# An attention and expert kernel planned over five engines: planned idle time of TensorE filled, single load buffers, timed priorities, and batch 0's q products turned by TensorE

## The chip, the cores and the metric

One core of a Trainium2 chip runs the whole program. The metric is the device time of one execution in microseconds (us), smaller is better. Times vary with the chip and from run to run, so a kernel is only compared with the kernel before on the same chip, in the same rounds.

Names of engines: PE is TensorE (matmul; PEld its weight load), DVE is VectorE, ACT is ScalarE, POOL is GpSimd, SP issues the DMAs. The time outside the profiled span is about 2 us (span 101.7 us in an execution timed at 103.5).

On one core a run is called "slow" when it is over 1.5% above the fastest run of the same kernel.

## The reference

```python
# q, k, v: (4 batches, 4 heads, 1088 rows, 32); S1, S2: (8, 32)
def phi(x):                                    # 64 features per head and row
    a = einsum('rd,bhsd->bhsr', S1, x)         # "sketch"
    b = einsum('rd,bhsd->bhsr', S2, x)
    return outer_product(a, b)                 # "product", 8 x 8
q_p, k_p = phi(q), phi(k)
kv  = einsum('bhsf,bhsd->bhfd', k_p, v)        # "k-v"
num = einsum('bhsf,bhfd->bhsd', q_p, kv)       # "numerator"
den = q_p . sum_s(k_p) + 1e-6
x   = (num / den), heads side by side          # (4, 1088, 128)
# then one expert of 8 for each batch:
e   = argmax(mean_s(x) @ w_gate); g = softmax(...)[e]          # "gate"
out = g * (relu(x @ w1[e]) @ w2[e])            # w1 128x1024, w2 1024x128
```

So each batch is a chain: load, turn, sketch, products, k-v, numerator, mean, gate, load of the chosen weights, cast, two expert products, store. Four batches are independent, which is what the kernel uses to keep the engines busy.

## The kernel before

Every step is an operation with a cost for each engine that may run it, a priority, the operations that it waits for and the buffers that it uses. A list scheduler in the program plays the plan through in simulated time and fixes, when the kernel is built, the order of instructions on each engine, which of two engines runs a flexible step, and which buffer it gets. Hardware then runs each engine's list in that order and waits on semaphores. `big` is a pair of PSUM banks, `small` one bank; a `small` is half of a two-bank tile.

```python
    kinds = dict(kld=2, qld=2, vld=2, kT=2, qT=2, ...)        # buffers of each kind
    banks = [psum.tile([P, 2, 512], FP32, name=f"ps{i}") for i in range(4)]
    def T(slot):
        if slot.kind == "big":
            return banks[slot.index]
        if slot.kind == "small":
            return banks[slot.index // 2][:, slot.index % 2, :]
        ...
    # in attention(b, pr): 
        both = {"DVE": 0.97, "POOL": 1.52} if FLEX[b] else {"POOL": 1.52}
        kp = [add(both, products(kab, phk, s), ...) for s in range(3)]
        ...                                                    # [cut]
        qtr = []
        for s in range(3):
            pq = add(both, products(qab, phq, s), after=[iv], ...)
            qtr.append(add({"DVE": 0.95}, lambda s=s: nc.vector.transpose(...), after=[pq], ...))
        ...                                                    # [cut]
        def logits():
            for i in range(3):
                nc.tensor.matmul(T(lgps)[:, 0:E], T(pool)[:, i:i + 1].to_broadcast([P, P]), wg[:, :],
                                 start=(i == 0), stop=(i == 2))
    ...                                                        # [cut]
    FLEX = (True, False, False, False)
    A = (0, 100, 200, 300)           # priorities: batch after batch,
    M = (400, 500, 600, 700)         # experts after all attention
    with tc.manual_schedule():
        for op in plan.order():
            op.run()
```

Names in the profile: `kld qld vld` loaded inputs, `kT qT` turned inputs, `kab qab` sketches, `phk phq` products, `phT` turned q products, `wq` the weights of the q sketch, `wf wbf` expert weights in fp32 and bf16, `hT` hidden, `ob` output rows. All PSUM tiles are `ps`.

## Time and profile before

| | before |
|---|---|
| time, median of 4 runs beside the result | 103.4 us (102.97 to 104.7) |
| span of the profiled execution | 101.7 us |
| busy: PE, DVE, ACT, POOL | 78.3, 69.3, 37.6, 37.9 us |
| first expert matmul | 47.78 us |
| last product on POOL ends | 62.7 us |

The page of the kernel before: busy times, then the span in 40 slices with each engine's busy share in tenths.

```profile
...
PE 78.3 (77%) x1625; PEld 57.8 (57%) x1625; DVE 69.3 (68%) x126; ACT 37.6 (37%) x86; POOL 37.9 (37%) x40
...
PE   5894891688509995695999899589899989999810
...
POOL 6023400009990009896699999000140300000000
...
PE 50%; DVE 14%; POOL 9%; ACT 8%; issue 7%; DMA 6%; SPq 1%; DVEq 0%; ACTq 0%
...
```

No engine is full over the span, PE comes nearest. The row of PE has weak slices up to the 19th and is 8 or 9 in nearly all after that; POOL has holes of zeros before slice 16. The last line is the chain that ended last: half PE, the rest hops between engines.

The windows view of the kernel before says the same in numbers; columns are the stretch, its length, busy time (instructions) of PE, PEld, DVE, ACT and POOL, then the granted clock of PE, the DMA share and GB/s.

```profile
...
5.00:33.00 28.00, 18.30 (x455) 14.05 (x467) 18.30 (x28) 2.83 (x9) 10.17 (x8) 1.00 0.75 191
47.80:97.10 49.30, 45.30 (x768) 33.39 (x768) 37.68 (x70) 28.18 (x59) 17.14 (x12) 1.00 0.38 106
...
```

From 47.8 to 97.1 us PE is the limit (45.3 of 49.3). From 5 to 33 us nobody is. The granted clock reads 1.00 in both stretches, although the same group of matmuls takes 1.6 times as long early as late (below); so I read PE's speed from durations. Counts of matmuls are those of the profile, which has two records for each fp32 matmul of the code.

The groups view of the kernel before: busy time and mean ns after the first bar, then the idle time of the engine just before these instructions and what ended it.

```profile
...
L316 POOL TENSOR_TENSOR phk<-kab 128x768 f32<-128x768 f32 x10 | 16.6, 1673 | 22.6 <-ACT kab L286 19.3 <-DVE kab L288 3.3
...
L381 PE MATMUL ps<-phk,vld 128*32 128x64 f32 x288 | 8.7, 268 | 4.8 <-POOL phk L316 3.8 <-issue 0.5 <-DVE wq L363 0.4
...
```

POOL sat idle 22.6 us before its products of k, 19.3 of it waiting for ACT's copy of a k sketch. The timeline of the kernel before shows why (columns: start, duration, engine, operation, out<-in, and in brackets the idle time before it with what ended it).

```profile
...
9.20 2.15 POOL L316 TENSOR_TENSOR phk<-kab 128x768 f32<-128x768 f32 x1 [3.32 <-DVE kab L288]
...
13.30 2.29 PE L328 MATMUL ps<-wq,qT 128*32 128x96 f32 x49
...
18.70 1.18 PE L328 MATMUL ps<-wq,qT 128*32 128x96 f32 x23 [3.11 <-issue]
...
20.43 2.15 PE L328 MATMUL ps<-s,kT 128*32 128x64 f32 x72
...
23.04 3.72 POOL L316 TENSOR_TENSOR phk<-kab 128x768 f32<-128x768 f32 x2 [11.69 <-ACT kab L286]
...
```

Batch 0's q sketch starts at 13.30, stops after 49 of its 72 matmuls for 3.11 us in which the profile shows nothing that PE waits for ("issue"), and goes on at 18.70. Batch 1's k sketch stands behind it in PE's order and runs at 20.43, so POOL waits from 11.35 to 23.04 us.

### The profile page before, as it was taken

How to read it: one execution, taken by the hardware profiler on the slowest of the kernel's cores; microseconds unless marked ns; L12 is line 12 of the kernel's file. 1: busy time of each engine (PE TensorE's matmuls, PEld its weight loads, DVE VectorE, ACT ScalarE, POOL GpSimd, SP SyncE). 2: the span in 40 equal slices, each digit the busy share in tenths (PEclk: the TensorE clock that was granted, in tenths of full speed). 3: DMA queues.
4: the chain of work that ended last, by engine and by line, in shares of the span. 5: the costliest groups of instructions: out<-in, count | busy, mean ns of one | idle time of the engine just before them, and what ended most of it. 6: DMA issues, size and time to landing. Idle time of an engine off the chain costs nothing.

```text
span 101.7 us, 3774 instructions
## 1 busy us (share of the span) xinstructions
PE 78.3 (77%) x1625; PEld 57.8 (57%) x1625; DVE 69.3 (68%) x126; ACT 37.6 (37%) x86; POOL 37.9 (37%) x40
## 2 busy tenths in 40 slices
PE   5894891688509995695999899589899989999810
PEld 2283690476306673693567766457568767777600
DVE  2538860099986478929987876936986877998220
ACT  3202000122001532018946384527655645555200
POOL 6023400009990009896699999000140300000000
PEclk9999999999999999579999999999999999999995
DMA  2999999972402600860000259138655722222231
GB/s 51 340 257 274 296 242 335 204 193 55 186 0 58 165 3 0 241 188 6 0 6 0 67 96 325 37 71 259 205 151 190 235 65 63 71 66 57 66 82 41
DMA packets 11023, 13.35 MB, mean 131 GB/s; under 512 B 1536, under 2 KB 9216, under 8 KB 11008
## 3 DMA queue, kind: packets, MB, share of 16 engines
q1 hardware_dynamic: 10784, 13.11, 47.3%
q8 instruction: 12, 0.20, 0.8%
q10 hardware_dynamic: 224, 0.01, 0.1%
q14 instruction: 3, 0.02, 0.1%
HBM read 10.89 MB, written 2.23 MB: 129 GB/s over the span
## 4 chain that ended last, share of the span: by engine, by line
PE 50%; DVE 14%; POOL 9%; ACT 8%; issue 7%; DMA 6%; SPq 1%; DVEq 0%; ACTq 0%
PE ps L540 16%; PE ps L328 13%; POOL phk L316 7%; PE ps L519 7%; PE ps L449 7%; DMA qld<-in_q_dram 6%; ACT hT L529 5%; PE ps L381 4%; DVE ob L553 3%; DVE phT L438 3%; DVE hT L531 3%; POOL phq L316 2%; PE ps L475 2%; PE ps L393 2%; SPq L299 1%
## 5 line engine op out<-in xcount | busy, mean ns | idle before, releaser
L316 POOL TENSOR_TENSOR phk<-kab 128x768 f32<-128x768 f32 x10 | 16.6, 1673 | 22.6 <-ACT kab L286 19.3
L529 ACT ACTIVATE hT<-ps 128x768 bf16<-128x768 f32 (+1 forms) x26 | 19.4, 774 | 12.9 <-PE ps L519 12.9
L540 PE MATMUL ps<-wbf,hT 128*128 128x128 bf16 (+1 forms) x288 | 19.0, 219 | 1.9 <-ACT gate L487 0.8
L540 PEld LDWEIGHTS <-hT 128*128 128x128 bf16 (+1 forms) x288 | 17.0, 99 | 5.7 <-issue 3.7
L531 DVE TENSOR_SCALAR hT<-ps 128x768 bf16<-128x768 f32 (+1 forms) x22 | 19.3, 908 | 1.0 <-PE ps L519 0.9
L519 PE MATMUL ps<-xbf,wbf 128*128 128x384 bf16 (+1 forms) x96 | 18.3, 317 | 1.3 <-ACT wbf L286 0.6
L316 POOL TENSOR_TENSOR phq<-qab 128x768 f32<-128x768 f32 x10 | 15.6, 1584 | 2.3 <-DVE qab L432 1.9
L328 PE MATMUL ps<-wq,qT 128*32 128x96 f32 x288 | 10.1, 311 | 4.1 <-issue 3.1
L553 DVE TENSOR_SCALAR ob<-ps,gate 128x384 f32<-128x384 f32 (+2 forms) x15 | 7.3, 507 | 7.8 <-PE ps L540 6.4
L381 PE MATMUL ps<-phk,vld 128*32 128x64 f32 x288 | 8.7, 268 | 4.8 <-POOL phk L316 3.8
L519 PEld LDWEIGHTS <-wbf 128*128 128x128 bf16 x96 | 8.6, 99 | 6.2 <-issue 1.5
L328 PEld LDWEIGHTS ps<-wq,qT 128*32 128x32 f32 x288 | 8.8, 144 | 5.8 <-issue 4.3
L438 DVE STREAM_TRANSPOSE phT<-phq 128x768 f32<-128x768 f32 x12 | 11.3, 959 | 0.5 <-POOL phq L316 0.5
L381 PEld LDWEIGHTS ps<-phk,vld 128*32 128x32 f32 x288 | 6.4, 137 | 7.0 <-POOL phk L316 4.6
L288 POOL CAST wbf<-wf 128x1024 bf16<-128x1024 f32 x3 | 3.6, 1210 | 15.1 <-DMA wf<-in_moe_w_dram 9.6
L449 PE MATMUL ps<-phT,kvs 32*32 32x256 f32 (+1 forms) x256 | 7.1, 463 | 0.6 <-DVE phT L438 0.6
L328 PE MATMUL ps<-s,kT 128*32 128x64 f32 x288 | 6.9, 267 | 0.8 <-DVE s L267 0.7
L288 DVE COPY qab<-ps 128x256 f32<-128x256 f32 (+1 forms) x4 | 1.7, 439 | 8.5 <-ACT qab L286 6.9
L286 ACT COPY qab<-ps 128x320 f32<-128x320 f32 (+1 forms) x4 | 1.6, 414 | 15.9 <-PE ps L328 15.9
L305 DVE STREAM_TRANSPOSE kT<-kld 128x576 f32<-128x576 f32 (+1 forms) x8 | 5.6, 729 | 2.0 <-DMA kld<-in_k_dram 2.0
L305 DVE STREAM_TRANSPOSE qT<-qld 128x576 f32<-128x576 f32 (+1 forms) x8 | 5.6, 720 | 2.0 <-DMA qld<-in_q_dram 2.0
L328 PEld LDWEIGHTS ps<-s,kT 128*32 128x32 f32 x288 | 6.0, 141 | 1.6 <-issue 0.8
(62 smaller groups left out, 71.3 us busy)
## 6 DMA issues: line engine op xcount, KB each, us to landing
wf<-in_moe_w_dram SPq DMA_DIRECT2D x8, 512.0 KB, 4.3
out_dram<-ob SPq DMA_DIRECT2D x40, 48.0 KB, 1.6
kld<-in_k_dram SPq DMA_DIRECT2D x3, 544.0 KB, 8.5
qld<-in_q_dram SPq DMA_DIRECT2D x3, 544.0 KB, 7.9
vld<-in_v_dram SPq DMA_DIRECT2D x8, 144.0 KB, 7.7
vld<-in_v_dram SPq DMA_DIRECT2D x8, 128.0 KB, 6.7
kld<-in_k_dram SPq DMA_DIRECT2D x1, 288.0 KB, 2.9
qld<-in_q_dram SPq DMA_DIRECT2D x1, 288.0 KB, 4.6
```

The lines of the kernel that those rows point to most:

```text
L288: (nc.vector if eng == "DVE" else nc.gpsimd).tensor_copy(o, i)
L305: return [add({"DVE": 0.05 + 0.04 * 2 * n}, lambda a=a, n=n: nc.vector.transpose(out=T(tr)[:, 0:n, a:a + 2, :].rearrange("p c a t -> p a c ...
L316: (nc.vector if eng == "DVE" else nc.gpsimd).tensor_tensor(out=T(ph)[:, 3 * s:3 * s + 3, :, :].rearrange("p c h (i j) -> p (c h) i j", i=R ...
L328: nc.tensor.matmul(T(ps)[32 * a:32 * a + 32, c // n, w * (c % n):w * (c % n) + w], T(tr)[:, c, a, :], moving)
L381: nc.tensor.matmul(T(kvps)[32 * h:32 * h + 32, 0:64], T(vld)[:, h, c, :], T(phk)[:, c, h, :], start=(c == 0), stop=(c == NC - 1))
L438: qtr.append(add({"DVE": 0.95}, lambda s=s: nc.vector.transpose(out=T(phT)[:, :, 3 * s:3 * s + 3, :].rearrange("p f c t -> p c f t"), in_= ...
L449: nc.tensor.matmul(T(nps[a // 2])[32 * h:32 * h + 32, a % 2, 0:32 * LEN[a]], T(kvs)[32 * a:32 * a + 32, u, h, :], T(phT)[32 * a:32 * a + 3 ...
L519: nc.tensor.matmul(T(hp)[:, t, 0:w], T(wbf)[:, 0, 128 * j:128 * j + 128], T(xbf)[:, 384 * s:384 * s + w])
L529: nc.scalar.activation(out=o, in_=i, func=AF.Relu)
L531: nc.vector.tensor_scalar(out=o, in0=i, scalar1=0.0, scalar2=None, op0=MAXOP)
L540: nc.tensor.matmul(T(ops)[0:n, 128 * i:128 * i + 128], T(hT)[:, j, 128 * i:128 * i + n], T(wbf)[:, 1, 128 * j:128 * j + 128], start=(j == ...
L553: nc.vector.tensor_scalar_mul(T(ob)[0:n, lo:hi], T(ops)[0:n, lo:hi], g[0:n])
```

## The change

The intent: fill TensorE's planned idle time, use single load buffers, give each stage of each batch a tuned priority, and let TensorE turn batch 0's q products. The diff is long and holds more than its title says. Its core, with cuts marked:

```diff
-    kinds = dict(kld=2, qld=2, vld=2, ...
+    kinds = dict(kld=1, qld=1, vld=1, ...
                                             # [cut: the plan doubles PE costs before 8 us, adds 0.15 for a
                                             #  change of tile form, and models instruction pages of 256]
-                for a in range(4):          # k sketch: 72 matmuls into 32 rows
-                    nc.tensor.matmul(T(ps)[32 * a:32 * a + 32, ...], T(tr)[:, c, a, :], moving)
+                for o in range(0, P, m):    # 36 into 64 rows (m = 64); q sketch as before (m = 32)
+                    nc.tensor.matmul(T(ps)[o:o + m, ...], t[:, o:o + m], moving)
-        both = {"DVE": 0.97, "POOL": 1.52} if FLEX[b] else {"POOL": 1.52}
+        either, pool_only = {"DVE": 1.16, "POOL": 1.52}, {"POOL": 1.52}
+                if eng == "DVE" and ps is not None:     # one operand read from PSUM, not SBUF
+                    for c in range(3 * s, 3 * s + 3): ...
                                             # [cut: q products scaled straight out of PSUM, half of the q copies]
-            qtr.append(add({"DVE": 0.95}, ... nc.vector.transpose(...
+            tq = add({"PE": 0.7}, turn, ...)            # batch 0: 128-wide TensorE turns
+            te = add({"ACT": ..., "DVE": ...}, copy(eng, T(pT)..., T(tps)...))
+            nm = add({"PE": 0.66}, num, ...)            # numerator chunk by chunk
-            for i in range(3):                          # logits
-                nc.tensor.matmul(T(lgps)[:, 0:E], T(pool)[:, i:i + 1]...
+        sm = add({"DVE": 0.1}, ... reduce_sum(T(pool)[:, 3:4], ...))
+        lg = add({"PE": 0.3}, ... one matmul ...)
                                             # [cut: expert weights loaded and cast by halves; the first
                                             #  expert product waits for its own chunk of x alone]
-    FLEX = (True, False, False, False)
-    A = (0, 100, 200, 300)
-    M = (400, 500, 600, 700)
+    PT = (True, False, False, False)
+    FK = (False, True, False, True)
+    K = (-3.42, 23.86, 57.18, 51.88)        # [cut: nine more lines of tuned numbers]
+    def filler():
+        nc.tensor.matmul(T(wslot)[:, :], warm[:, 0:128], warm[:, :])
+    idle = plan.idle(ops, FILL)
-        for op in plan.order():
+        for op in ops:
             op.run()
+            for _ in range(int((idle.get(op, 0.0) - 0.1) / (0.43 if op.start < plan.COLD else 0.215))):
+                filler()
```

In the changed kernel's order there are 14 fillers.

## The prediction

> **What bounds it now.** Two stretches. From 47.8 us to 97.1 us TensorE is the limit: the windows view shows it busy 45.3 of 49.3 us, and the chain of waits runs mostly through the two expert products (24 second-product matmuls take 1.45-1.5 us, eight first-product ones 1.2-1.4). Before that nothing is full: from 5 to 33 us PE is busy 18.3 of 28, DVE 18.3, POOL 10.2. The chain there hops between loads, POOL and PE. POOL, which needs 32 us for its 20 feature products, idles 22.6 us before its phk products, 19.3 of it waiting for the ACT copy of the k sketch, and ends its last product at 62.7.
>
> PE is also slow there. The timeline shows 24 k-v matmuls in 0.87 us at 10-31 us and in 0.54 us from 40 us on; the k sketch takes 2.15 us at 5 and 20 us, about 1.3 us (estimate from 55 of 72 in 0.98) at 36 us. The Trainium skill, "TensorE: Matmul & The Clock Gate", Part 1, says an idle PE runs at half clock until some 3.4 us of sustained work; the trace's 1.6 times fits. PE further stops 3.1 us in the middle of a q sketch (15.6-18.7), waiting for nothing shown: probably instruction fetch queued behind loads (inferred).
>
> **What the change does.**
> - Fillers keep PE busy through planned gaps (14 dummy matmuls, 0.43 us cold, an estimated 0.22 warm) and should make PE warm from about 8 us instead of 33.
> - Single load buffers limit outstanding loads to three, so instruction pages queue behind less.
> - Timed priorities interleave batches. The order shows POOL nearly without holes (phk0, phk1, phq0, phq1, phk3/phk2, phq2, weight casts, phq3).
> - Batch 0 loses three DVE transposes (0.96 us each) and four DVE products (1.6-2.0 us each); gains PE transposes and three ACT copies of about 0.8 us. Two products (b1, b3) move to DVE reading one operand from PSUM. The Trainium skill, "SBUF — State Buffer", says a DVE instruction with two SBUF inputs contends with GpSimd reads; here POOL products took 2.2 us beside DVE's and 1.5 alone.
> - Three logits matmuls become one: about 4 x 0.5 us off PE.
>
> **Sum.** POOL starts at about 8; phk0 and phk1 to about 17, phq0 to 21.5. Batch 0 then needs turn, copy, numerator, gate (about 5 us) and weights plus cast (47.8 - 38.9 = 9 us before, some 8 now): first expert matmul at about 34.5, was 47.8. After it remain the expert work (12 x 1.48 + 12 x 1.33 = 34 us) and attention left over (q3, kv2, two numerators, turns, gates: about 8 us), plus 4 us of stalls as before, and the 4.6 us tail of eviction and store: 34.5 + 34 + 8 + 4 + 4.6 = 85 us of span, and 2 us between span and measured time: **87 us, 82 to 95**. Chances: faster by over 2% 0.94, within 2% 0.03, slower 0.03.
>
> **What would show it.** K-v groups of 0.54 us from before 15 us; no 3 us PE stop; POOL's last product before 48 us (62.7); first expert matmul at 31-38 us; from there PE over 90% busy; DVE busy 55-62 us (69.3), ACT over 42 us (37.6).
>
> **What would make it wrong.** PE cools again between fillers; instruction pages still stall it (more instructions early); single buffers starve POOL; ACT holds gate or weight copies behind others; fillers sit in front of work that is ready.

## The result, and the profile after

A ratio is the mean time of one kernel's fast runs over the mean of the other's fast runs of the same rounds, so it is not quite the ratio of the medians quoted beside it.

| | before | after |
|---|---|---|
| time, median of 4 runs each | 103.4 us | 93.91 us (93.49 to 94.58) |
| ratio of fast runs | | 0.910 (95%: 0.902 to 0.918) |
| span | 101.7 | 92.0 us |
| first expert matmul | 47.78 | 39.02 us |
| last product on POOL ends | 62.7 | 55.4 us |
| DVE busy | 69.3 | 56.7 us |

The page after, the same lines:

```profile
...
PE 76.6 (83%) x1453; PEld 55.5 (60%) x1456; DVE 56.7 (62%) x127; ACT 42.6 (46%) x89; POOL 37.8 (41%) x41
...
PE   4988999886999879969997989999869968899600
...
POOL 6022970999497999129922890040000000000000
...
PE 56%; DMA 13%; DVE 11%; POOL 6%; ACT 3%; issue 3%; SPq 3%; DVEq 0%; ACTq 0%
...
```

The windows view after, with the stretch that begins at its own first expert matmul:

```profile
...
5.00:33.00 28.00, 24.67 (x571) 18.99 (x572) 18.72 (x47) 8.37 (x27) 20.11 (x17) 1.00 0.63 188
39.00:87.40 48.40, 42.38 (x688) 30.84 (x688) 32.98 (x67) 30.37 (x55) 11.98 (x9) 1.00 0.45 118
...
```

Early PE went from 18.3 to 24.7 busy of 28 and POOL from 10.2 to 20.1. In the late stretch PE is busy 42.4 of 48.4, so it stands idle 6.0 us there.

The timeline after, early part:

```profile
...
5.58 0.23 DVE L289 TENSOR_TENSOR s<-ps,mask 128x64 f32<-128x64 f32 x1 [0.60 <-PE ps L677]
...
11.42 2.76 PE L365 MATMUL ps<-wq,qT 128*32 128x96 f32 x72
...
14.01 0.51 PE L417 MATMUL ps<-phk,vld 128*32 128x64 f32 x24
...
14.44 1.27 PE L365 MATMUL ps<-s,kT 128*64 128x64 f32 x36
...
16.16 2.98 POOL L352 TENSOR_TENSOR phk<-kab 128x768 f32<-128x768 f32 x2 [3.00 <-ACT kab L308]
...
19.10 1.51 POOL L352 TENSOR_TENSOR phq<-qab 128x768 f32<-128x768 f32 x1
19.52 0.19 DVE L399 TENSOR_TENSOR wq<-ps,mask 128x32 f32<-128x32 f32 x1 [1.09 <-PE ps L677]
...
```

The q sketch of batch 0 runs in one piece (2.76 us, no stop), the k-v group of 24 takes 0.51 us at 14.0 us (0.87 as late as 30 us before), and POOL waits 3.00 us for batch 1's k sketch where it waited 11.69. Two lines show a new cost: `s` and `wq` on DVE wait for L677, a filler.

The groups view after answers the two lines of before:

```profile
...
L352 POOL TENSOR_TENSOR phk<-kab 128x768 f32<-128x768 f32 x10 | 14.8, 1513 | 5.8 <-ACT kab L308 3.6 <-DVE kab L310 2.2
...
L417 PE MATMUL ps<-phk,vld 128*32 128x64 f32 x288 | 6.0, 228 | 2.1 <-POOL phq L352 0.7 <-DVE gate L567 0.7 <-DMA vld<-in_v_dram 0.4
...
```

From the PE groups of both profiles one can see where PE's own time went: the k-v groups fell from 8.7 to 6.0 us, the q sketches from 10.1 to 9.0, the logits from 3.1 to 1.5. Without warm-up (3.2 us in both) and fillers (3.9 us of records), PE worked 75.1 us before and 69.5 after; the rest of the span, in which it did nothing useful, fell from 26.6 to 22.5 us.

The timeline after, where batch 0 reaches its gate:

```profile
...
28.09 2.46 PE L365 MATMUL ps<-s,kT 128*64 128x64 f32 x72
...
30.47 0.39 PE L559 MATMUL ps<-wg,pool 128*128 128x8 f32 x2
...
31.52 0.17 DVE L565 MAX8 gate<-ps 128x8 f32<-128x8 f32 x1 [0.28 <-PE ps L391]
...
```

Batch 0's x (the input of its experts) is complete at 29.2 us, but its logits (L559) stand in PE's order behind 72 k-sketch matmuls of batches 2 and 3, and start at 30.47.

The waits view after, PE from 39 to 87.4 us (columns: us in total, times, longest), and the end of the timeline:

```profile
...
PE ps L631 <- ACT ob L641: 1.6, 3, 0.9
PE ps L631 <- DVE ob L644: 1.5, 2, 0.8
...
```

```profile
...
83.60 1.95 PE L631 MATMUL ps<-wbf,hT 128*128 128x128 bf16 x32
...
85.59 0.62 DVE L644 TENSOR_SCALAR ob<-ps,gate 128x384 f32<-128x384 f32 x1 [1.05 <-PE ps L631]
86.26 1.05 PE L631 MATMUL ps<-wbf,hT 128*128 128x128 bf16 x16 [0.71 <-DVE ob L644]
...
```

The second expert product (L631) waits for the eviction of the group before (`ob`), 0.71 us in the last case. The plan gives every group another PSUM bank, but after the change it alternates between the two banks of one tile, and the semaphores order accesses by tile. Before the change the plan rotated among four tiles.

### The profile page after: what moved, and what is told of

Read it like the earlier page. It is cut to its first block, busy times and chain, and to the rows that moved or that the text cites. A ratio compares the mean times of both kernels' runs of the same rounds, so it can differ in the third digit from the quotient of the medians.

```text
span 92.0 us, 3442 instructions
## 1 busy us (share of the span) xinstructions
PE 76.6 (83%) x1453; PEld 55.5 (60%) x1456; DVE 56.7 (62%) x127; ACT 42.6 (46%) x89; POOL 37.8 (41%) x41
## 4 chain that ended last, share of the span: by engine, by line
PE 56%; DMA 13%; DVE 11%; POOL 6%; ACT 3%; issue 3%; SPq 3%; DVEq 0%; ACTq 0%
PE ps L631 19%; PE ps L610 10%; PE ps L365 10%; DMA vld<-in_v_dram 7%; DMA qld<-in_q_dram 6%; DVE ob L644 5%; PE ps L417 5%; PE ps L505 4%; POOL phk L352 3%; POOL phq L352 3%; PE ps L533 3%; PE ps L540 2%; ACT ob L641 2%; SPq L321 1%; SPq L410 1%
## 5 line engine op out<-in xcount | busy, mean ns | idle before, releaser
L620 ACT ACTIVATE hT<-ps 128x768 bf16<-128x768 f32 (+1 forms) x30 | 22.0, 781 | 7.7 <-PE ps L610 7.7
L631 PE MATMUL ps<-wbf,hT 128*128 128x128 bf16 (+1 forms) x288 | 20.0, 219 | 3.8 <-ACT ob L641 1.6
L631 PEld LDWEIGHTS <-hT 128*128 128x128 bf16 (+1 forms) x288 | 17.8, 99 | 7.9 <-issue 6.0
L352 POOL TENSOR_TENSOR phq<-qab 128x768 f32<-128x768 f32 x12 | 17.8, 1514 | 6.7 <-DVE qab L483 6.7
L622 DVE TENSOR_SCALAR hT<-ps 128x768 bf16<-128x768 f32 (+1 forms) x18 | 16.2, 905 | 5.0 <-PE ps L610 4.9
L352 POOL TENSOR_TENSOR phk<-kab 128x768 f32<-128x768 f32 x10 | 14.8, 1513 | 5.8 <-ACT kab L308 3.6
L496 DVE STREAM_TRANSPOSE phT<-phq 128x768 f32<-128x768 f32 x9 | 8.4, 956 | 0.1
L417 PE MATMUL ps<-phk,vld 128*32 128x64 f32 x288 | 6.0, 228 | 2.1 <-POOL phq L352 0.7
L644 DVE TENSOR_SCALAR ob<-ps,gate 128x384 f32<-128x384 f32 (+2 forms) x10 | 4.7, 492 | 5.0 <-PE ps L631 4.9
L365 PEld LDWEIGHTS ps<-s,kT 128*64 128x64 f32 x144 | 5.4, 159 | 1.9 <-DVE s L289 1.2
L365 PE MATMUL ps<-s,kT 128*64 128x64 f32 x144 | 5.9, 248 | 0.3 <-DVE s L289 0.3
L308 ACT COPY kab<-ps 128x384 f32<-128x384 f32 (+1 forms) x6 | 2.2, 402 | 7.4 <-DVE kab L310 5.5
```

Of the source, the lines that this page charges most:

```text
L352: (nc.vector if eng == "DVE" else nc.gpsimd).tensor_tensor(out=T(ph)[:, 3 * s:3 * s + 3, :, :].rearrange("p c h (i j) -> p (c h) i j", i=R ...
L365: nc.tensor.matmul(T(ps)[o:o + m, c // n, w * (c % n):w * (c % n) + w], t[:, o:o + m], moving)
L417: nc.tensor.matmul(T(kvps)[32 * h:32 * h + 32, 0:64], T(vld)[:, h, c, :], T(phk)[:, c, h, :], start=(c == 0), stop=(c == NC - 1))
L496: turns = [add({"DVE": 0.95}, lambda s=s: nc.vector.transpose(out=T(phT)[:, :, 3 * s:3 * s + 3, :].rearrange("p f c t -> p c f t"), in_=T( ...
L620: nc.scalar.activation(out=o, in_=i, func=AF.Relu)
L622: nc.vector.tensor_scalar(out=o, in0=i, scalar1=0.0, scalar2=None, op0=MAXOP)
```

## The experiments

"Ratio" is that of medians over all rounds; the last column has that of the fast means.

| run | what | median us | fast mean | before: median, fast mean | ratio of medians | of fast means |
|---|---|---|---|---|---|---|
| nofill | after without fillers | 94.52 | 92.01 | 103.76, 100.29 | 0.911 | 0.917 |
| before_fill | before with fillers (wrong result) | 102.52 | 101.67 | same | 0.988 | 1.014 |
| fillapart | after, early results in tiles of one bank | 91.42 | 90.25 | same | 0.881 | 0.900 |
| apart | after, accumulators in tiles of one bank | 90.71 | 89.05 | same | 0.874 | 0.888 |
| after_again | after | 92.69 | 92.48 | 102.65, 99.60 | 0.903 | 0.929 |
| both_apart | both splits | 88.47 | 88.27 | same | 0.862 | 0.886 |
| oldprio | after with the old priorities | 92.53 | 91.60 | same | 0.901 | 0.920 |
| before_fill2 | before with fillers, mended | 103.67 | 99.02 | same | 1.010 | 0.994 |
| b0dve | oldprio, batch 0 back on DVE | 97.06 | 96.77 | 101.68, 100.41 | 0.955 | 0.964 |
| rot | after with load buffers doubled | 97.15 | 96.83 | same | 0.955 | 0.964 |
| unnamed | all the title's parts undone | 98.98 | 98.21 | same | 0.973 | 0.978 |
| bothapart_nofill | both splits, no fillers | 87.84 | 87.65 | same | 0.864 | 0.873 |

The changed kernel itself has 0.908 and 0.903 of medians, 0.910 and 0.929 of fast runs, so a difference of less than about 0.02 (2 us) says nothing. A theory and its rivals: I held at first that the order of the work (timed priorities and what the plan makes of them) made the gain; the rivals were the fillers and the warm clock, then the freed VectorE, the load buffers, and the small forms that the title does not name.

### nofill: do the fillers make the gain?

```diff
-            for _ in range(int((idle.get(op, 0.0) - 0.1) / (0.43 if op.start < plan.COLD else 0.215))):
-                filler()
```

> The changed kernel without its 14 filler matmuls; every other instruction and its order stay. Changed: 93.9 us. Theory CLOCK (the fillers buy PE's full clock early, and that is much of the gain): k-v groups of 24 take 0.87 us until 25 us or later instead of from 14 us on, q sketch of batch 1 2.7 us instead of 1.7, time 96 to 99 us. Rival ORDER (the order of work buys the gain, PE warms by the dense real work): k-v groups at 0.54 us from about 15 to 20 us all the same, time 92 to 94.5 us, perhaps below the changed kernel because s12 and wq no longer wait behind fillers (0.6 and 1.1 us in the changed trace).

Measured: 94.52 us, ratio 0.911, beside 0.908 and 0.903 for the changed kernel in its two series. Timeline of the kernel without fillers:

```profile
...
12.31 3.14 PE L365 MATMUL ps<-wq,qT 128*32 128x96 f32 x72
...
16.02 1.82 PE L365 MATMUL ps<-s,kT 128*64 128x64 f32 x36
...
```

PE is slow until about 17 us: the q sketch takes 3.14 us, the k sketch of 36 matmuls 1.82 where it takes 1.27 with the full clock. In the changed kernel's profile it came at about 14 us. But the moment varies without any change of fillers: the k sketch at 5.6 us took 2.19 us in the profile of the changed kernel and 1.27 in that of after_again, the same kernel; unnamed, which has no fillers, has 1.27 at 5.3 us, and bothapart_nofill, also without, has its fast k-v group of 0.51 us at 13.9. So that fillers bring the full clock forward is not shown. What is shown is that taking them out changes the time by less than the calls resolve.

### before_fill and before_fill2: fillers alone, on the kernel before

```diff
+    plan.add({"PE": 0.0}, lambda: None, after=[sts[1]["nm"]], prio=-30, uses=[wslot])
+            for _ in range(int((idle.get(op, 0.0) - 0.1) / (0.43 if op.start < plan.COLD else 0.215))):
+                filler()
```

> The kernel before with its order kept to the instruction on every engine, plus 37 filler matmuls in PE's planned gaps up to 30 us. Before: 103.4 us. Theory CLOCK: warm from about 14 us, 18 us of half-clock PE work before 33 us shrinks by some 6 us, of which half lies on the chain: 99 to 101 us. Rival ORDER: the early part is set by loads, POOL and waits; PE gets warm but the time stays within 1.5 us of 103.4.

before_fill gave a wrong result: my fillers went on writing after their PSUM bank had been given to other work. Its 102.52 us settles nothing. The mended kernel keeps the bank for as long as fillers run (28 of them):

> The kernel before with 28 fillers, mended: all of them ahead of the first numerator, so that none writes a PSUM bank that has been given to other work (the first attempt wrote on after that, and its result was wrong). Order kept on every engine. ORDER: 101.5 to 103.5 us with a correct result, k sketches at 1.2 us from about 16 us on where they took 2.15. CLOCK: 98 to 100.5.

Measured: correct, 103.67 us, ratio 1.010. Fillers alone gain nothing on the kernel before. Its timeline shows that the long stop stayed, and grew:

```profile
...
18.50 1.49 PE L334 MATMUL ps<-wq,qT 128*32 128x96 f32 x28 [4.52 <-issue]
...
23.58 1.51 POOL L322 TENSOR_TENSOR phk<-kab 128x768 f32<-128x768 f32 x1 [11.99 <-ACT kab L292]
...
```

PE had its full clock from about 11 us to the stop in this run (44 matmuls of the q sketch in 1.16 us, where before took 2.29 for 49), so it only reached its stop earlier. The stop is 4.52 us long, and after it the k sketch takes 2.15 us again, at the slow clock. POOL's products of batch 1 start at 23.58 (23.04 before).

### fillapart: do the fillers hold back work through a shared tile?

```diff
-    banks = [psum.tile([P, 2, 512], FP32, name=f"ps{i}") for i in range(4)]
+    # slots 0 and 1 (the fillers' bank and its neighbour): one-bank tiles until the first `big` use of pair 0
+    for j in (0, 1):
+        single[j] = fp.tile([P, 512], FP32, name=f"one{j}")
```

> The changed kernel with the fillers' PSUM bank in a tile of its own: same instructions, same order, but the DVE mask of s12, the DVE mask of wq and the ACT copy of zs no longer wait for fillers that write the other bank of the same tile. Theory SHARED TILE: s12 done at about 5.2 instead of 5.8 us, wq of batch 1 at 18.4 instead of 19.7, the first expert matmul 0.5 to 1.5 us earlier, time 92.5 to 93.5. Rival: POOL and the weights set the pace and nothing moves: 93.9 plus or minus 0.4.

Measured: 91.42 us, ratio 0.881 against 0.903 to 0.908. The order of instructions is unchanged. Timeline:

```profile
...
5.23 0.19 DVE L296 TENSOR_TENSOR s<-one,mask 128x64 f32<-128x64 f32 x1
...
16.41 0.18 DVE L406 TENSOR_TENSOR wq<-one,mask 128x32 f32<-128x32 f32 x1
...
17.44 1.69 PE L372 MATMUL ps<-wq,qT 128*32 128x96 f32 x72
...
```

The time is below the range that I gave (92.5 to 93.5). The two lines that waited for a filler after the change (`s` at 5.58, `wq` at 19.52) now stand at 5.23 and 16.41, without a wait. So the fillers did hold back work in the neighbouring bank. But most of these 3.1 us are not theirs, as PE was slow until 14 us in that profile and fast from about 10 in this one. after_again, the changed kernel with PE as fast as here (q sketch of 1.67 us at 10.5 in both), has `wq` at 17.65, waiting 1.26 us for a filler, and its first expert matmul at 38.09 us, fillapart at 36.81: about 1.3 us. The medians say 2 to 3. If the fillers only held work back by so much, nofill should have gained it; it did not, and in the split form (bothapart_nofill) taking them out costs nothing that would balance it. So the size stays open.

### apart: does the shared tile cost time in the expert stretch?

```diff
+    # after the last `big` use of pair 2: its two banks become two tiles
+                for j in (4, 5):
+                    single[j] = late.tile([P, 512], FP32, name=f"one{j}")
```

> The changed kernel with the two PSUM banks of the output accumulators as two tiles from the point on where they are used singly: same instructions, same order. In the changed trace PE waits 3.9 us for output evictions (1.6 ACT ob, 1.5 DVE ob, 0.4 pool, 0.4 before the logits), though the matmul that waits writes the other bank. Theory SHARED TILE: these waits fall below 1 us, PE over 92% busy from 39 us on (87.6% now), time 90.5 to 92. Rival (PE would wait anyway, for the relu copies that feed it): time 93.5 plus or minus 0.5, the waits reappear under hT.

Measured: 90.71 us, ratio 0.874. The waits of L631 for `ob` are gone from the list, and PE is busy 39.9 of 42.1 us from 39 us to its last matmul. Its profiled run also had a full clock from 5.4 us on, which belongs to the run and not to the edit, so of the difference in single profiles not all is the edit's; the medians over six runs are what counts.

### both_apart beside the changed kernel again: do the two add up?

> The changed kernel itself, on the chip of the other runs of this call, as their yardstick. Every theory: 93.9 us give or take 1; its fast runs at 0.91 of those of the kernel before.

> The changed kernel with both PSUM pairs as separate tiles (the fillers' pair early, the accumulators' pair late), order kept. The first runs gave about 2.5 us for the one and 3.3 for the other, in medians. Theory SHARED TILE (two separate causes, in separate stretches): the savings add, 88 to 89.5 us. Rival (the chip and the clock of those runs were luckier): 91 to 93 us.

Measured on one chip: 92.69 and 88.47 us (fast means 92.48 and 88.27), so 4.2 us, in the range of the theory that they add, though less than the 5.8 us that I had put together from the first runs. In the same place of the timeline as above:

```profile
...
77.58 2.84 PE L640 MATMUL one<-wbf,hT 128*128 128x128 bf16 x48
...
79.12 0.62 DVE L653 TENSOR_SCALAR ob<-one,gate 128x384 f32<-128x384 f32 x1 [0.31 <-DMA out_dram<-ob]
...
```

The 48 matmuls of the last two groups run through in one piece, while DVE evicts the first of them beside. The result is correct. The first expert matmul comes at 37.39 us and PE is busy 40.9 of the 44.3 us after it.

### oldprio: do the tuned priorities make the gain?

```diff
-    K = (-3.42, 23.86, 57.18, 51.88)     # and the nine other lines of tuned numbers
+    K = (0, 100, 200, 300)               # numbers of the kernel before, in the new places
```

> The changed kernel with the priorities of the kernel before (each batch 100 after the last, experts from 400, second products right after their first, w and v loads as before); fillers, single load buffers, TensorE turns and the planner's new costs stay. Theory ORDER: most of the 9.5 us goes, 98.5 to 102 us, POOL's last product after 55 us, first expert matmul after 42 us. Rival (the smaller mechanisms, products out of PSUM, turns on TensorE, one logits matmul, make the gain): 94 to 96.5 us.

Measured: 92.53 us, ratio 0.901 (after_again 0.903). My theory fell here (98.5 us or more), and the time is below the rival's range too (94 to 96.5). With the plain priorities of before, everything else as changed, the time is the same. The order does differ (first expert matmul at 41.50 instead of 39.02 us), and is worth nothing in the end: PE waits 1.1 us for `ob` in its list, 3.5 after the change; its profile fell in a slow run, so I take no more from it. Whether the tuned priorities gain something once the tiles are split was not run.

### rot: do single load buffers gain anything?

```diff
+        if slot.kind in ("kld", "qld", "vld"):       # two buffers in turn; order of every engine kept
+            if not hasattr(slot, "half"):
+                turns[slot.kind] = turns.get(slot.kind, -1) + 1
+                slot.half = turns[slot.kind] % 2
+            return bufs[slot.kind][slot.half]
```

> Edit: the changed kernel with the order of every engine kept, but each load buffer (k, q, v) doubled and used in turn, so a load no longer waits for the turn of the batch before it. Theory LOADS (single buffers gain by keeping few loads in flight, so that loads land in 4 us instead of 8 and instruction fetch is not held up): loads land in 6 us or more, a stop of 1.5 us or more in the middle of a PE group comes back before 30 us, time 95.5 us or more, ratio to before 0.93 or more. Rival (single buffers gain nothing, they save memory only): ratio 0.895 to 0.915, as the changed kernel, and k loads of batches 1 to 3 issued earlier.

Measured: 97.15 us, ratio 0.955 of medians and 0.964 (0.957 to 0.972) of fast runs. All of what the theory of the loads said came: k, q and v loads land in 7.1, 6.2 and about 5.5 us (4.9, 3.7 and about 3.6 after the change), and the stop is back. Timeline:

```profile
...
12.84 1.20 PE L372 MATMUL ps<-s,kT 128*64 128x64 f32 x33
...
18.23 0.33 PE L372 MATMUL ps<-s,kT 128*64 128x64 f32 x3 [4.18 <-issue]
...
18.99 1.51 POOL L359 TENSOR_TENSOR phk<-kab 128x768 f32<-128x768 f32 x1 [5.56 <-ACT kab L315]
...
```

Batch 1's k sketch starts at 12.84, 1.6 us earlier than in the changed kernel because this run's clock was full, and stops before its last 3 matmuls for 4.18 us. POOL gets it at 18.99 (16.16 after the change), the first expert matmul comes at 42.50 us (39.02). PE's useful work was even less than in the changed kernel (65.9 us: 73.9 less 3.2 warm-up and 4.8 fillers), the time it did nothing useful was 29.0 us instead of 22.5. So having the second load buffers costs 3 to 5 us (96.83 less the fast means 93.97 and 92.48 of the changed kernel, or the ratios of medians 0.955 less 0.903 and 0.908), through the stop, and not because the loads themselves come late: the turns of batch 1's k start at 11.44 us here and 11.07 in the changed kernel.

The DMA view of this run for 15 to 16 us, inside the stop:

```profile
...
q1 hardware_dynamic: 127, 0.26, 105.9%
q8 instruction: 1, 0.02, 8.0%
...
```

The load queue takes the whole time of the 16 engines in this microsecond, and one transfer of instructions lies in it. The kernel before has the same picture at 15 to 16 us, inside its own stop. That the stop is PE waiting for its next page of instructions behind the loads fits this and is likely; the profile does not name the receiver of the page, so it is argued and not shown. One more thing speaks for it: the place of the stop. The windows view from 0 to just before the stop, of before, before_fill2 and rot in this order, counts what PE and PEld had done:

```profile
...
0.00:18.69 18.69, 11.93 (x222) 7.99 (x222) 9.00 (x15) 2.26 (x5) 4.42 (x18) 1.00 0.95 253
...
0.00:18.49 18.49, 11.35 (x222) 6.25 (x222) 9.19 (x15) 2.26 (x5) 4.42 (x18) 0.96 0.94 267
...
0.00:18.22 18.22, 10.37 (x222) 6.50 (x222) 8.44 (x20) 2.40 (x5) 6.74 (x20) 1.00 0.93 267
...
```

All three stop after 222 weight loads and 222 matmuls, though they are then at different work (49 or 44 matmuls into a q sketch, 33 into a k sketch); unnamed and apart stop (2.41 and 0.54 us) after 222 weight loads and 221 recorded matmuls. The later stops of 1.3 to 1.8 us in rot, apart, fillapart, both_apart and bothapart_nofill (at 35.9 to 41.6 us) all come after 730 weight loads; bothapart_nofill has 14 fillers fewer than both_apart and stops 14 matmuls further into the same group. A place that is fixed in the count of instructions, and not in the work, is what a page of instructions would give. The first transfer of the queue `instruction` after the start begins at 15 to 17 us in before, before_fill2, rot and unnamed, just before 12 us in the changed kernel, which passes the same place without a stop. What is shown over all runs: in the first 25 us the kernels with double load buffers stop 3.1 (before), 4.5 (before_fill2), 4.2 (rot) and 2.4 us (unnamed), and 1.4 in before_fill; the single-buffered ones with the old tiles (after, nofill, after_again, oldprio, b0dve) 0.4 us or less. With single buffers and split tiles there are still stops of 0.3 to 1.8 us, most of them later.

### b0dve: does freeing VectorE of batch 0 make the gain?

```diff
-    PT = (True, False, False, False)
+    PT = (False, False, False, False)
-        kp = [add(either if FK[b] else pool_only, products(kab, phk, s, kps), ...
+        kp = [add(both if b == 0 else ..., products(kab, phk, s, kps if FK[b] else None), ...
+        # the same for qp; on top of the old priorities
```

> Edit: the old-priorities version of the changed kernel (92.5 us, ratio to before about 0.90), and batch 0 given back to VectorE as before the change: its k and q products free to go to DVE or POOL from SBUF (the plan puts two phk and two phq products on DVE), its q products turned by DVE in 32 blocks, no TensorE turns, no copies of turns by ACT. Fillers and single load buffers stay. Theory RELIEF (freeing VectorE of batch 0 makes the gain; DVE busy went from 69.3 to 56.7 us): at least 97 us, ratio to before 0.95 or more, POOL products at 2.1 us beside DVE's, first expert matmul at 44 us or later. Rival FORMS (the many small things make it: logits in one matmul, weights loaded and cast by halves, products scaled straight out of PSUM, two k products of batches 1 and 3 on DVE from PSUM): at most 94.5 us, ratio at most 0.925, first expert at 43 us or earlier. In favour of the rival: TensorE turns cost PE 2.6 us which this run saves.

Measured: 97.06 us, ratio 0.955 of medians, 0.964 (0.955 to 0.972) of fast runs; oldprio had 0.901 of medians and 0.920 of fast runs, so the ratio rose by 0.054 or 0.044, about 5 us. Timeline:

```profile
...
20.10 1.09 DVE L346 TENSOR_TENSOR phk<-ps,kab 128x256 f32<-128x256 f32 x3 [1.70 <-ACT kab L308]
...
20.15 1.51 POOL L352 TENSOR_TENSOR phk<-kab 128x768 f32<-128x768 f32 x1 [8.51 <-ACT kab L308]
...
21.54 3.13 DVE L352 TENSOR_TENSOR phq<-qab 128x768 f32<-128x768 f32 x2
21.70 2.16 POOL L352 TENSOR_TENSOR phq<-qab 128x768 f32<-128x768 f32 x1
...
```

The four lines show the two forms. DVE's product of batch 1 (L346, one operand from PSUM, three instructions) takes 1.09 us beside a POOL product of 1.51. Batch 0's on DVE (L352, both operands in SBUF) take 3.13 us for two (0.95 for the first, 2.27 for the second, which overlap in the records), and the POOL product beside them 2.16. This agrees with the Trainium skill, "SBUF — State Buffer", § Who interferes with whom: a DVE instruction with two SBUF inputs contends with a GpSimd instruction that reads SBUF, one with at most one does not.

In time the theory of relief held, in its mechanism only in part. I had expected batch 0 itself to be late, with a first expert matmul at 44 us or later; it came at 39.61. The loss lies behind it: the stretch from there to 92.0 us is 52.4 us long with 46.5 us of PE work (48.4 and 42.4 after the change). While POOL idles 8.51 us and is slowed, less of the later batches' attention is done before the experts begin. This run also has 26 fillers and another order, and its profile fell in a slow run, so the 5 us belong to the package of batch 0, not to one instruction. A part of POOL's wait is even the fillers': batch 1's k sketch is done at 17.9 us, but ACT waits 2.25 us, to 19.09, for a group of five of them at 17.80 before it gets to the copy that POOL needs.

### unnamed: all that the title names undone at once

```diff
-    kinds = dict(kld=1, qld=1, vld=1, ...
+    kinds = dict(kld=2, qld=2, vld=2, ...
     # and no fillers, old priorities, batch 0 on DVE as in b0dve
```

> Edit: everything that the change's title names is undone at once in the changed kernel: no fillers, load buffers doubled, old priorities, batch 0 back on DVE (products free between DVE and POOL, turns by DVE). What stays is what the title does not name: 64-wide k sketch, one logits matmul, q products scaled straight out of PSUM with half the copies, expert weights loaded and cast by halves, first product waiting for its chunk alone, k products of batches 1 and 3 free to go to DVE from PSUM, new costs in the plan. Theory NAMED (the four named parts together make the gain): 100 us or more, ratio to before 0.97 or more. Rival FORMS (the unnamed parts make it): 96 us or less, ratio 0.935 or less. Between the two: both have a share, which is then read off as the distance to 1 and to 0.905.

Measured: 98.98 us, ratio 0.973 of medians, 0.978 (0.969 to 0.987) of fast runs. It falls between the two theories, nearer to the one of the named parts. Of the distance from 1 to 0.905, 0.068 of 0.095 or about 70% goes with the named parts, and some 2 to 3 us stay with the small forms. Since fillers and priorities gained nothing when each was undone alone, the named parts that count are the load buffers and batch 0. Each alone is worth about 5 us, both together about 7: they overlap. A likely reason is that both make POOL wait for batch 1's k sketch (5.56 us in rot, 8.51 in b0dve, 9.29 here, 3.00 in the changed kernel).

### bothapart_nofill: do fillers help when they block nothing?

> Edit: the version with its PSUM accumulators and its early small results in tiles of one bank each (88.5 us, ratio to before 0.862), order kept, without its 14 fillers. Theory (fillers do help once they no longer hold back work on the neighbouring bank: without them the clock is full later, as in the run without fillers, where it came at 17 us): ratio 0.88 or more, about 90.5 us; k sketch at 5 us 1.8 us or longer and k-v groups of 0.87 before 15 us. Rival (fillers are worth nothing in either form): ratio 0.855 to 0.87, 87.5 to 89 us.

Measured: 87.84 us, ratio of medians 0.864 (both_apart 0.862). The full clock does come later in this profile, as the first theory had it (k sketch at 5.35 us 2.19 us, k-v 0.87 at 10.99; in the profile of both_apart 1.27 and 0.87), but the time is in the range of the rival. The ratio of fast runs, 0.873 (0.866 to 0.880), lies between the two ranges; but both_apart has 0.886 by the same measure, so nothing points to a gain from the fillers. I read this as: a worth of the fillers is not shown. The simplest version that beats both kernels is this one: the changed kernel with split tiles and without fillers, about 4 us below the changed kernel.

## Why the prediction was right or wrong, point by point

The time was inside the range, 93.9 for a point of 87.0, and the direction was right. Of the signs: k-v groups of 0.54 us before 15 us (right, 0.51 at 14.0); no 3 us stop (right); POOL's last product before 48 us (wrong, 55.4); first expert matmul at 31 to 38 us (wrong, 39.0); from there PE over 90% busy (wrong, 42.4 of 48.4 is 88%); DVE 55 to 62 us (right, 56.7); ACT over 42 us (right, 42.6).

**The sum.** "34.5 + 34 + 8 + 4 + 4.6 = 85 us of span" came out as 39.0 + 42.4 + 6.0 + 4.6 = 92.0. The work term was right (42 for 42.4). Two terms were mis-sized:

- "First expert matmul at about 34.5" was 39.0. Batch 0's q products ended at 23.56, not 21.5: POOL started at 8.71 instead of about 8, and it waited 3.00 us for batch 1's k sketch, which stands behind batch 0's q sketch in PE's order: "POOL nearly without holes" was read from the order of POOL alone. From there to the gate it took 8.5 us and not "about 5": the logits stood 1.1 us behind 72 sketch matmuls of other batches, and the evictions are three in a row. The weights took 7.0 and not 8.
- "4 us of stalls as before" was 6.0. The second product waits for `ob` of the group before, through a tile shared by two banks. An order list does not show this wait, as it does not tell which banks share a tile. Taking it and the early shared tile away gives 88.5 us, near to the 87 of the sum, though not by the sum's terms: the first expert matmul is still at 37.4 us and not at 34.5.

**The causes.** "Fillers ... should make PE warm from about 8 us instead of 33": PE was warm from about 14 us in the profile of the changed kernel and from about 5 in after_again, but runs without fillers spread as widely (5 to 17 us), so the clock part is not shown; and as a cause of the gain it was wrong, as nofill (0.911), before_fill2 (1.010) and bothapart_nofill show. PE's speed was not what the early stretch waited for. "Timed priorities interleave batches": they do, and oldprio shows that this is worth nothing here. "Single load buffers limit outstanding loads to three, so instruction pages queue behind less": right in its effect (the page of instructions stays inferred), and under-weighted: rot shows 3 to 5 us. "Batch 0 loses three DVE transposes and four DVE products": right as a large part, about 5 us in b0dve, though the loss without it falls in later batches. "Three logits matmuls become one: about 4 x 0.5 us off PE": PE's logits fell by 1.6 us; it was not tested alone.

What the Trainium skill, "TensorE: Matmul & The Clock Gate", Part 1, says of a cold and a warm PE agrees with the traces in direction (24 k-v matmuls in 0.87 and then 0.51 to 0.54 us, a ratio of 1.6 and not 2), also that the moment varies from run to run: with the same order of instructions the k sketch at 5.4 to 5.9 us took 2.19 (after), 1.90 (fillapart) and 1.27 us (apart, both_apart, rot).

What stays open: that the stop is an instruction page of PE (its place in the count of instructions speaks for it); how large the hold-back by the fillers is; how the 5 us of batch 0 divide into POOL's slowing, the DVE transposes and the order; and which of the unnamed forms hold the last 3 us.

## What to carry to other kernels

Before filling an engine's idle time ask what the stretch waits for: on the kernel before, PE had its full clock at 11 us instead of 33 (but for the time from its stop to about 24 us) and the time did not move, while in the changed kernel undoing the single load buffers, or the relief of VectorE from batch 0, cost 3 to 5 us each. Where semaphores follow tiles, two accumulators in one tile are one buffer; give each its own tile before tuning the order. When a change has many parts, undo each alone and all together, for the parts need not add up.

## What the Trainium skill lacked or had wrong

- "Runtime: NRT & Kernel Launch", § Instruction fetch mechanics, says that the cost of crossing a block of instructions is "mostly hidden". In this program, if the stops are that, it is not hidden while many loads are in flight: PE stopped 3.1 us (before), 4.5 (before_fill2) and 4.2 us (rot) inside one group of matmuls, each time after 222 weight loads and with an instruction transfer inside the stop, and 0.4 us or less with single load buffers and the tiles as they were. The page says nothing of loads delaying instructions.
- "PSUM — Partial Sum Buffer", § PSUM bank collisions raise a hardware error, gives the rule to guard PSUM by bank and quadrant. Eviction of one bank beside matmuls into another ran correct in both_apart. It lacks the price of guarding more coarsely: two pairs of banks, each ordered as one tile, cost 4.2 us of 92.7.
- "TensorE: Matmul & The Clock Gate", Part 1, advises against idle gaps of PE. No page says that warming PE is worth nothing where PE is not what is waited for: without fillers 94.52 us at a ratio of 0.911, with them 0.903 to 0.908.
- "SBUF — State Buffer", § Who interferes with whom, had the rule right; it gives no size for this pair of instructions. Here, in b0dve, the first DVE product takes 0.95 us, the POOL product begun within it 2.16 instead of 1.51, the second DVE product 2.27 and the next POOL product 2.22. The four end 4.5 us after the first began (21.54 to 26.04), where one after the other they would take 4.9 (estimate: twice 0.95 and twice 1.51), so little is gained by running them side by side. The DVE form with one operand in PSUM takes 1.09 us beside a POOL product that stays at 1.51.
